# Building a structured matrix by angle addition, and re-timing the loads around it, in a fused S4 + ReGLU training step

## The chip, the cores, the metric

One core of one Trainium2 chip. The metric is the device time of the core in microseconds (us). TensorE is PE in the profile, VectorE DVE, ScalarE ACT, GpSimd POOL, SyncE SP.

## The reference, cut to what matters

`x` is 2048 rows of 576 features. The output is `x` plus two branches of its layernorm, and the kernel returns that output and the gradients of twelve inputs for a given `grad_out`.

```
xn = layernorm(x)
# S4 branch: one long filter per feature, applied by FFT over the rows
dt = exp(log_dt); logdA = dt*(A_re + i A_im); dB = dt*(B_re + i B_im)
K  = Re sum_n C[d,n] * exp(logdA[d,n] * l) * dB[d,n]          # l = 0..2047
y  = irfft(rfft(xn, 4096) * rfft(K, 4096))[:2048] + xn * Dskip
# feed-forward branch, 576 -> 4608 -> 576
h  = relu(xn @ W_gate) * (xn @ W_up);   z = h @ W_down
out = x + y + z
```

## The kernel before: what the change and the argument touch

Two streams of work are written as Python generators and woven into one program. The feed-forward stream runs over 12 chunks of 384 hidden columns and gives PE most of its work. The S4 stream runs beside it: parameters; pass 1 over features 0 to 287 ("half 0"); then making the filter of half 0 beside pass 1 of half 1; making the filter of half 1 beside pass 3 of half 0; pass 3 of half 1. A number that each piece yields, its assumed time, sets the pace at which the two are mixed.

```python
def gen(self):                                   # S4
    yield from self.params()
    self.make_dft16(); yield 1.0
    yield from self.make_dft128()
    with ExitStack() as c:
        pools = self.p2_pools(c)
        yield from self.p1(0)
        yield from self.both(self.p2(0, pools), 0.8 * W2, self.p1(1), W1)
        yield from self.both(self.p2(1, pools), 0.8 * W2, self.p3(0), W3)
    yield from self.p3(1)
    yield from self.grads()                      # parameter gradients, at the end
```

The FFT is split into two steps with a turn through DRAM between them: rows are stored in one order and read in the other. The loads are issued where they are used, with two buffers.

```python
bp = self.pool(c, f"p1_b{hf}", 2)                # pass 1, middle part
for h in range(ST):
    b = bp.tile([P, 2, 2, DH], BF16, name="b_ug")
    nc.sync.dma_start(b[:], self.rows(self.A[2][hf], h))     # the other order
    ...                                          # matmuls (mix)
    Z = self.product(pp, sg[:, 1], sg[:, 0], True)           # DVE
    Ct = bp.tile([P, 1, 2, DH], BF16, name="fC1")
    self.back1(Ct, 0, Z)                                     # matmuls on that product
    nc.sync.dma_start(self.rows(self.C[1][hf], h), Ct[:])
```

The filter needs Y, a complex exponential on a grid of 128 exponents. For four features at a time it is computed directly: angle, range reduction, sine, absolute value, cosine, times the decay.

```python
v.tensor_tensor(E[:], ex[:, es, 16:24]..., ex[:, es, 24:40]..., op=ALU.mult)
v.tensor_tensor(ya[:], par[1]..., qv..., op=ALU.mult)
v.tensor_scalar(yr[:], ya[:], MAGIC, None, op0=ALU.add)
v.scalar_tensor_tensor(yr[:], yr[:], MAGIC, ya[:], op0=ALU.subtract, op1=ALU.subtract)
nc.scalar.activation(sn[:], yr[:], ACT.Sin, scale=-TWO_PI)
nc.scalar.activation(ya[:], yr[:], ACT.Abs)
nc.scalar.activation(cs[:], ya[:], ACT.Sin, scale=-TWO_PI, bias=g.hpcol[:])
v.tensor_tensor(Y[:, 0], Ef, cs[:], op=ALU.mult)
v.tensor_tensor(Y[:, 1], Ef, sn[:], op=ALU.mult)
```

In the feed-forward stream, twelve transposes (three tiles of four) run in a bunch through two PSUM buffers, and the chunk's gate, up and down weights have two copies, loaded half a chunk ahead from ScalarE's queue.

```python
def t_unit(self, c, sg, ft):
    for src, dst in zip(self.T[(c, sg, ft)], (self.hN, self.dgN, self.duN)):
        pt = g.psum_t.tile([P, 8, P], BF16, name="pt")       # pool of 2
        for j in range(JS):
            nc.tensor.transpose(out=pt[:, j, :], in_=src[:, j * P:(j + 1) * P], ...)
        g.bal.copy(dst[...], pt[:, 0:JS, :], 512, fp32=False)    # DVE or ACT

def load_wd(self, c):
    for i in (2, 0, 1):
        self.g.nc.scalar.dma_start(self.wds_[c % 2][:, i], self.Wd_in[c][:, i])
```

## Time and profile before

| | before |
|---|---|
| median, lowest, highest of 4 runs | 1968.49, 1966.09, 1975.11 us |
| span of the profiled run, granted clock | 1971.6 us, 0.978 |
| PE busy, idle | 1799.4, 172.2 us |
| DVE busy, ACT busy | 1412.0, 1355.9 us |

Read the PE row as span minus busy: that idle time is what a change outside PE's own work can reach. The lines themselves, and what is lost inside "busy", are in the prediction below.

### The profile page before, as it was taken

The page shows a single profiled execution, that of the slowest core. Times are in us where ns is not written, and L with a number is a line of the kernel's source. Part 1 is how long each engine was busy: PE and PEld are TensorE (multiplying, and loading weights), DVE is VectorE, ACT ScalarE, POOL GpSimd, SP SyncE. Part 2 cuts the span into 40 slices and gives each one's busy share as a digit, 9 for nine tenths or more (in the row PEclk, how much of TensorE's full clock was granted, in tenths as well). Part 3 has the DMA queues.
Part 4 walks back from the last instruction along what each step waited for, and adds up shares of the span by engine and source line. Part 5 has one row for each costly group of instructions (what it writes and reads, how often), then busy time and mean ns, then how long its engine had stood idle before and what let it go on. Part 6 is the DMA issues. An engine that isn't in the chain of part 4 may idle for free.

```text
span 1971.6 us, 42743 instructions
## 1 busy us (share of the span) xinstructions
PE 1799.4 (91%) x16257; PEld 1225.3 (62%) x16395; DVE 1412.0 (72%) x3521; ACT 1355.9 (69%) x3058; POOL 225.3 (11%) x276
## 2 busy tenths in 40 slices
PE   6879897999999999999899999999999998996999
PEld 3555565556766766766656756766766755564666
DVE  8746772699778688688577887868888833746882
ACT  2775683698779679679668769859868836644342
POOL 2111110012101011011101101101201200100000
PEclk9989998999999999999899999999999999998999
DMA  9688888766756756856856755755755656885874
GB/s 340 204 310 264 238 220 238 230 200 130 222 147 146 229 138 142 240 152 135 227 184 128 196 167 125 181 173 136 181 180 107 158 188 183 204 220 149 276 245 126
DMA packets 205961, 377.62 MB, mean 192 GB/s; under 512 B 34810, under 2 KB 115834, under 8 KB 203706
## 3 DMA queue, kind: packets, MB, share of 16 engines
q1 hardware_dynamic: 172922, 284.35, 44.4%
q0 software_dynamic: 25344, 54.28, 18.5%
q10 hardware_dynamic: 7488, 36.24, 5.2%
q8 instruction: 128, 2.10, 0.4%
q14 instruction: 79, 0.65, 0.1%
HBM read 235.29 MB, written 139.50 MB: 190 GB/s over the span
## 4 chain that ended last, share of the span: by engine, by line
PE 42%; DVE 19%; ACT 19%; DMA 14%; issue 4%; SPq 1%; POOL 0%; ACTq 0%; DVEq 0%; POOLq 0%
PE ps_mm L202 10%; PE ps_mm L250 9%; PE ps_mm L299 9%; PE ps_mm L286 3%; ACT osx L66 3%; DMA rows<-in_gq_dram 2%; PE ps_s L572 2%; PE pt L226 2%; DMA A_k<-fA 2%; ACT YT L66 2%; PE ps_s L806 2%; ACT hN L66 2%; PE ps_s L573 2%; DVE pr L822 1%; DMA bC<-C_dk 1%
## 5 line engine op out<-in xcount | busy, mean ns | idle before, releaser
L202 PE MATMUL ps_mm<-xT,wd 128*128 128x512 bf16 x1308 | 346.9, 384 | 8.0 <-DVE xT L139 1.0
L202 PEld LDWEIGHTS <-wd 128*128 128x128 bf16 x2160 | 204.0, 98 | 200.4 <-issue 14.6
L66 ACT CAST osx<-ps_mm 128x288 bf16<-128x288 f32 x658 | 255.9, 439 | 32.3 <-PE ps_mm L250 31.1
L260 POOL DMA_DIRECT2D acc_dram<-osx x160 | 138.7, 869 | 1156.4 <-ACT osx L66 805.4
L250 PE MATMUL ps_mm<-wf,dgT 128*128 128x288 bf16 x1152 | 215.8, 289 | 12.3 <-ACT osx L66 9.8
L250 PE MATMUL ps_mm<-wf,duT 128*128 128x288 bf16 x1152 | 216.5, 290 | 0.0
L299 PEld LDWEIGHTS <-rows 128*128 128x128 bf16 x1536 | 147.2, 98 | 96.7 <-issue 6.2
L250 PE MATMUL ps_mm<-wf,hT 128*128 128x288 bf16 x1152 | 192.8, 289 | 4.9 <-ACT osx L66 3.6
L202 PE MATMUL ps_mm<-gT,wd 128*128 128x512 bf16 x714 | 183.6, 379 | 0.3
L822 DVE TENSOR_TENSOR pr<-X,ps_s 128x256 f32<-128x256 f32 x288 | 109.1, 415 | 96.2 <-PE ps_s L818 95.0
L286 PE MATMUL ps_mm<-rows,hN 128*128 128x144 bf16 x2304 | 160.9, 231 | 14.2 <-DMA rows<-in_gq_dram 14.0
L286 PEld LDWEIGHTS <-hN 128*128 128x128 bf16 x2304 | 153.4, 100 | 22.7 <-issue 14.4
L209 DVE SCALAR_TENSOR_TENSOR upm<-rg,ps_mm 128x512 bf16<-128x512 bf16 x144 | 98.3, 683 | 92.7 <-PE ps_mm L202 74.0
L66 ACT COPY YT<-ps_s 128x1024 bf16<-128x1024 bf16 x142 | 145.9, 1028 | 26.8 <-PE ps_s L806 24.8
L299 PE MATMUL ps_mm<-dgN,rows 128*128 128x384 bf16 x768 | 144.2, 326 | 0.2 <-ACT rg L207 0.2
L250 PEld LDWEIGHTS <-dgT 128*128 128x128 bf16 x1152 | 112.5, 99 | 44.4 <-issue 14.8
L299 PE MATMUL ps_mm<-duN,rows 128*128 128x384 bf16 x768 | 137.0, 326 | 0.0
L250 PEld LDWEIGHTS <-duT 128*128 128x128 bf16 x1152 | 112.5, 99 | 28.9 <-issue 1.0
L250 PEld LDWEIGHTS <-hT 128*128 128x128 bf16 x1152 | 107.6, 99 | 36.2 <-issue 7.8
L66 ACT CAST dhb<-ps_mm 128x512 bf16<-128x512 f32 x144 | 84.7, 588 | 54.7 <-PE ps_mm L202 54.1
L66 ACT CAST obw<-ps_mm 128x384 bf16<-128x384 f32 x105 | 50.0, 478 | 102.8 <-PE ps_mm L299 83.3
L750 ACT ACTIVATE ycs<-ya,hpcol 128x512 bf16<-128x512 f32 x144 | 107.7, 748 | 2.9 <-DVE Y L753 2.1
(223 smaller groups left out, 3690.3 us busy)
## 6 DMA issues: line engine op xcount, KB each, us to landing
acc_dram<-osx POOLq DMA_DIRECT2D x176, 288.0 KB, 4.7
xT<-xT_dram SPq DMA_DIRECT2D x44, 640.0 KB, 5.4
gT<-in_gT_dram SPq DMA_DIRECT2D x44, 640.0 KB, 6.2
rows<-in_gq_dram SPq DMA_DIRECT2D x48, 576.0 KB, 4.9
rows<-xs_dram SPq DMA_DIRECT2D x48, 512.0 KB, 5.2
wd<-in_Wd_dram ACTq DMA_DIRECT2D x36, 480.0 KB, 6.9
wf<-in_Wf_dram ACTq DMA_DIRECT2D x12, 1296.0 KB, 9.1
ex_dram<-exs SPq DMA_DIRECT2D x18, 640.0 KB, 3.5
```

The costliest lines, as they stand in the source:

```text
L66: self.nc.scalar.copy(out, in_)
L202: nc.tensor.matmul(ps[:], lhsT=w[:, k, fs], rhs=rhs[:, k, :], start=(k == 0), stop=(k == NK - 1))
L209: nc.vector.scalar_tensor_tensor(upm[:], rg[:], 0.0, ps_u[:], op0=ALU.is_gt, op1=ALU.mult)
L226: nc.tensor.transpose(out=pt[:, j, :], in_=src[:, j * P:(j + 1) * P], identity=g.ident_bf[:])
L250: nc.tensor.matmul(ps[:, :DH], lhsT=lt, rhs=rh, start=(i == 0), stop=(i == len(mms) - 1))
L260: nc.gpsimd.dma_start(g.acc_dram[:, t, :, :], o[:], accum_op=ALU.add)
L286: nc.tensor.matmul(ps[:, (ft - f) * 144:(ft - f + 1) * 144], lhsT=self.hN[:, st, ft * P:(ft + 1) * P], rhs=gq[:, st, :], start=(st == 0), ...
L299: nc.tensor.matmul(ps[:, :Fc], lhsT=xs[:, st, 0:P], rhs=src[:, st, :], start=(st == 0), stop=(st == ST - 1))
L572: nc.tensor.matmul(ps[:, :DH], lhsT=CC[:], rhs=src[:, o, :], start=True, stop=False)
L573: nc.tensor.matmul(ps[:, :DH], lhsT=sm[:], rhs=src[:, other, :], start=False, stop=True)
L750: nc.scalar.activation(cs[:], ya[:], ACT.Sin, scale=-TWO_PI, bias=g.hpcol[:])
L822: nc.vector.tensor_tensor(pr[:], X[:, dx:dx + DG, r0:r0 + 2].rearrange("p d r a -> p d (r a)").unsqueeze(2).to_broadcast(sh), psg[:, 0:DG ...
```

## The change

Its intent: cut the work of DVE and ACT in making Y, and take away places where PE stands still for a round trip through DRAM, a PSUM buffer or a queue. Cut to the core (cuts are marked with ...):

```diff
 # making Y: by angle addition, Y = U + V, from small factors A (8 steps) and B (16 steps)
-E, ya, yr, sn, cs, Y as above: 6 DVE and 3 ACT instructions of 512 columns per 4 features
+A = [xop.tile([P, SX, 2, 8, 2], BF16, ...) for i in range(2)]    # once per 16 features
+B = xop.tile([P, SX, 2, 16], BF16, name="B")
+...
+v.tensor_tensor(vw(U), Ap(0), Bp(1), op=ALU.mult)                # per 4 features
+v.tensor_tensor(vw(V), Ap(1), Bp(0), op=ALU.mult)
+v.tensor_tensor(Y[:], U[:], V[:], op=ALU.add)
 # loads run ahead of use; the product of step h and the inverse of step h-1 are interleaved
+class Ahead: ...                       # keeps n loads in flight
-yield from self.p1(0)
+yield from self.both(self.p1(0, 4, 4.0), 68.0, self.params(pw), 45.0)    # depth 4, pause 4.0
-... self.p1(1) ... self.p3(0)
+... self.p1(1, 2, 0.0) ... self.p3(0, 2, 0.0)
-yield from self.p3(1)
-yield from self.grads()
+yield from self.p3(1, 4, 4.0)
 # the second DFT table is turned on PE from the first (32 transposes), not computed
 # the parameters come transposed from the host; gradients follow each filter half
+yield from self.param_grads(hf, Sm, pw, xp, yop)                         # end of p2
 # feed-forward: one bunch of 4 transposes after each group of matmuls
-def t_unit(self, c, sg, ft): ...
+def t_steps(self, units): ... yield
+    for _ in turns: next(src)
 # one copy of the weights, loaded at the chunk's start from SyncE's queue (chunk 0: ScalarE's)
-self.g.nc.scalar.dma_start(self.wds_[c % 2][:, i], self.Wd_in[c][:, i])
+(self.g.nc.scalar if c == 0 else self.g.nc.sync).dma_start(self.wd[i][:], self.Wd_in[c][:, i])
-PACE = 0.9
-W1, W2, W3 = 56.0, 400.0, 62.0
+PACE = 0.86
+W1, W2, W3 = 60.0, 400.0, 58.0
```

The "pause" is a piece of the S4 stream that does nothing: feed-forward work fills it while the store before the turn lands.

## The prediction

Its first rival is that U and V take 1.2 us each, not the 0.69 that it counts on, and load DVE. Its times for DVE's new instructions, and so its 78 us less on DVE, are the author's estimate: no DVE row of the kernel before multiplies or adds 1024 columns. The rows that come nearest allow both figures, again as estimates. In bf16 288 columns take 301 ns (L584) and 576 take 453 (L581), which puts 1024 at some 690 by a straight line; in fp32 512 columns take 684 ns (L743) and 1280 take 1490 (L515), which puts 1024 at some 1220.

Three things that it uses without a row are in the trace of the kernel before. A transpose takes 57 ns and a tiny matmul 24 in a run of eight (it counts 56 and 25):

```profile
1012.52 0.19 PE ps_s L796 x8
1012.71 0.46 PE ps_s L806 x8
```

And one wait cost more than its length: in the 2.7 us after the one of 4.79 us that the prediction shows (124.6 to 127.3 us), the granted clock was 0.50 and three matmuls of 288 columns took 0.88 to 0.92 us; from 128.95 us on three took 0.53 or 0.54. After a wait of 2.04 us at 133.37 us it was 1.00, and they took 0.53.

> **What bounds the kernel now.** I read the page's busy shares first, then the windows view by stage, then TensorE's waits, the chain of waits, the groups by form and one stretch of the timeline.
>
> ```profile
> PE 1799.4 (91%) x16257; PEld 1225.3 (62%) x16395; DVE 1412.0 (72%) x3521; ACT 1355.9 (69%) x3058; POOL 225.3 (11%) x276
> ```
>
> TensorE leads, but a busy PE is not a PE at its peak, so I ask how long its matmuls would take back to back. The chain of waits has dense runs:
>
> ```profile
> 59.38 2.60 PE ps_mm L202 x12
> ...
> 69.81 2.82 PE ps_mm L250 x23
> ...
> 1931.88 12.00 PE ps_mm L286 x192
> 1943.88 20.80 PE ps_mm L299 x128
> ```
>
> That is 216 ns for 512 columns, 123 for 288, 62.5 for 144, 162.5 for 384. Counting from the source: 2160 x 216 = 467 us, 3680 x 123 = 453, 2304 x 62.5 = 144, 1536 x 162.5 = 250, 384 half-width matmuls that run in pairs 31; for the S4 half 1024 x 123 = 126, 2960 transposes x 56 = 166, 2304 tiny ones x 25 = 58. Together 1695 us. The span is 1971.6, so some 277 us are lost: 172 as idle (1971.6 - 1799.4), some 105 inside "busy" (restarts, and a lower granted clock). The windows view says where (columns: stretch, then busy us and count of PE, PEld, DVE, ACT, POOL, then clock, DMA share, GB/s):
>
> ```profile
> 0.00:16.00 16.00, 0.00 (x0) 0.00 (x0) 9.94 (x45) 1.90 (x4) 2.10 (x12) 1.00 0.89 348
> ...
> 100.00:220.00 120.00, 101.72 (x774) 65.20 (x779) 66.58 (x124) 79.42 (x158) 17.25 (x33) 0.96 0.85 286
> 220.00:360.00 140.00, 117.27 (x888) 78.37 (x895) 71.09 (x194) 76.95 (x195) 13.61 (x15) 0.93 0.82 226
> 360.00:940.00 580.00, 551.95 (x5399) 380.79 (x5444) 473.26 (x1112) 470.63 (x1063) 72.11 (x75) 0.99 0.65 173
> ...
> 1000.00:1600.00 600.00, 573.25 (x5643) 399.39 (x5690) 469.88 (x1136) 464.41 (x1043) 76.74 (x80) 1.00 0.63 161
> 1600.00:1760.00 160.00, 147.59 (x1154) 94.62 (x1160) 80.29 (x247) 93.17 (x240) 13.80 (x16) 0.98 0.75 201
> 1760.00:1824.00 64.00, 46.40 (x292) 27.18 (x294) 38.00 (x157) 28.39 (x65) 1.07 (x2) 0.85 0.55 158
> ```
>
> PE idle is 41 us in 100 to 360 (parameters, DFT tables, first S4 pass), 55 in the two long middle stretches, where DVE and ACT are both near 80%, and 30 in 1600 to 1824 (last S4 pass and parameter gradients). What ended PE's idle time:
>
> ```profile
> PE ps_s L602 <- DMA bC<-C_dk: 14.8, 7, 6.9
> PE ps_mm L286 <- DMA rows<-in_gq_dram: 14.0, 8, 3.4
> PE ps_mm L250 <- ACT osx L66: 13.4, 10, 4.8
> PE pt L226 <- ACT hN L66: 13.0, 24, 4.2
> PE ps_s L561 <- ACT fA L66: 12.6, 12, 5.4
> ...
> PE ps_s L98 <- DVE dld L870: 6.3, 1, 6.3
> ```
>
> Latencies, then: a DRAM round trip, a PSUM buffer, an in-order queue behind another's wait. The timeline shows the last kind:
>
> ```profile
> 121.22 3.02 DVE L515 TENSOR_TENSOR exs<-Tt,ev 128x1280 f32<-128x1280 f32 x2 [4.24 <-DMA ex_dram<-exs]
> ...
> 124.68 0.88 PE L250 MATMUL ps_mm<-wf,dgT 128*128 128x288 bf16 x3 [4.79 <-ACT osx L66]
> ```
>
> DVE waits for a store to free exs, ACT's Exp waits for DVE, the PSUM copies of the feed-forward part queue behind that Exp, and PE, which needs their buffers, stands still for 4.79 us.
>
> [...] the gappy stretches have clocks of 0.93 and 0.85, the dense ones 0.99 and 1.00. So a removed gap saves more than its length. [...]
>
> **The change, part by part.** PE's matmuls stay: the instruction streams differ by 32 new transposes of 56 ns and some 40 small ones gone. The 1695 us floor stands, and only the lost 277 can shrink.
>
> *Making Y.* Per four channels the old code spends three ACT and six DVE instructions, among them:
>
> ```profile
> L748 ACT ACTIVATE ysn<-yr 128x512 bf16<-128x512 f32 x144 | 94.7, 658 | 11.7 <-DVE yr L745 10.7 <-DVE Y L754 0.4
> L743 DVE TENSOR_TENSOR ya<-Tt,qv 128x512 f32<-128x512 f32 x144 | 98.3, 684 | 5.8 <-ACT ycs L750 5.4
> ```
>
> All six DVE groups: 98.7 + 98.3 + 61.9 + 98.7 + 66.8 + 60.1 = 484.5 us. ACT's three: 94.7 + 95.1 + 107.7 = 297.5. The new code builds Y by angle addition, Y = U + V, from small factors: 3 x 144 bf16 instructions of 1024 columns[...]. The per-16-channel block grows: angles for 40 exponents instead of 16[...]. Its three ACT instructions grow from 1.43 to 2.39 us by the row slope (256 to 512 columns costs 216 ns): +35. Net: DVE -78, ACT -262.
>
> *Parameters and gradients.* With the host's transposed layout no PE transposes, no R and T round trips, half the trigonometry of the DFT tables: about DVE -30, ACT -20. So DVE ends near 1300, ACT near 1080. This is off PE's path; it shortens the answers to PE.
>
> *Waits.* Idle saved, stage by stage:
> - 60 to 360 (46 us idle): exs gets three buffers and is spread over the first S4 pass; the pass prefetches four deep, pipelines product and inverse by one step, and puts a pause of feed-forward work before each DRAM turn-around. I give 28 of the 46: the store-to-load turn itself remains.
> - Middle (360 to 1600, 65 us with the entry of the second pass at 940 to 1000): feed-forward transposes no longer come three in a row on two PSUM buffers, but one after each matmul group (13.6 us of hN and duN waits); a lighter ACT answers sooner. Against it the gate, up and down weights lose their second copy and load at the chunk's start on SyncE's queue, ahead of the rows that already cost 14.0. I give 20 - 5 = 15.
> - 1600 to 1824 (30 us): the gradients leave the end (6.3 for dld, the R loads, stores at L473 and L849), the last pass prefetches four deep: 18.
> - Final stage (8 us): 2.
>
> Sum 63. Each idle us came with 105/172 = 0.6 us of hidden loss; since part of that is fixed, I take 0.55: 63 x 1.55 = 98. From 1968.5 that gives 1870; with 2 us for the new transposes, **1872 us**, 4.9% less.
>
> **Rivals.**
> [...] Sums and feed-forward products answer later and the middle gains nothing or loses: about 1915. For it: four-dimensional operands with repeats, seen in no row. Against: yE already repeats a word sixteen times at 687 ns, no slower than plain rows[...].
> *Single weights turn into the wait.* 1.44 MB more at each of 11 chunk starts is some 4 us at the 340 GB/s that the page's fullest slices reach. About 20 us of final products and down-gradients lie ahead of first use, so gate and up are hidden, but rows queue behind them. If 2 to 3 us show at each start: +25, about 1895.
> *The middle does not care.* Its idle is 4.5%, in hundreds of short waits, and PE, DVE and ACT share out latency. If only start and end gain, (28 + 18 + 2) x 1.55 = 74: about 1895.
> *More than I think.* If nearly all hidden loss goes and the middle's idle halves: about 1840.
>
> **Range and chances.** The first and last stages alone carry it past the 2% line (1929), whatever the middle does, unless U and V are slow and the weights stall too. 8 in 10: 1838 to 1915. Faster by over 2%: 0.91; within 2%: 0.08; slower: 0.01.
>
> **What would show it.** U, V and Y near 690 ns each (1.2 us refutes it); ACT busy near 1080, DVE near 1300; PE idle near 110 us; the 100 to 360 stretch without a 4 us wait on osx; waits of pt on hN under 4 us; no R or dld row, and final products starting some 90 us earlier. New waits of L200 on wd, or rows waits well above 14 us, would speak for the second rival. If PE idle fell and time did not, the hidden part would be wrong.

## The result, and the profile after

The changed kernel takes **1884.01 us** (median of 10 runs, 1880.80 to 1889.69) against 1968.51 (15 runs, 1966.09 to 1976.94). The ratio is 0.9565, with a 95% interval of 0.9549 to 0.9581: 4.35% less. Ratios here are the mean time of one kernel's fast runs over that of the other's of the same rounds, so not quite the ratio of the medians. All outputs are right.

The profiled run spans 1886.4 us at a clock of 0.988. The page's first part, to be read against the line of before at the head of the prediction:

```profile
PE 1764.8 (94%) x16248; PEld 1218.4 (65%) x16389; DVE 1335.8 (71%) x3059; ACT 1162.0 (62%) x2599; POOL 217.3 (12%) x264
```

PE idle is 1886.4 - 1764.8 = 121.6 us, 50.6 less than before. The span fell by 85.2, so each idle microsecond brought 1.68. ACT is far lighter, DVE a little.

The windows view of the changed kernel (stretch, then busy time and count of PE, PEld, DVE, ACT, POOL, then clock, DMA share, GB/s). The stretches are cut where the S4 stream changes stage in that trace: the first pass writes out its result (dk) at 346 us in the kernel before and at 279 us now.

```profile
0.00:285.00 285.00, 243.92 (x1823) 159.22 (x1845) 199.74 (x505) 176.92 (x385) 41.41 (x78) 0.98 0.85 285
285.00:1510.00 1225.00, 1168.65 (x11460) 815.61 (x11554) 912.79 (x1999) 808.49 (x1814) 159.13 (x167) 0.99 0.66 173
1510.00:1740.00 230.00, 220.74 (x1904) 151.08 (x1919) 130.96 (x353) 121.56 (x295) 16.74 (x20) 0.99 0.76 224
1740.00:1846.00 106.00, 95.01 (x709) 65.71 (x714) 86.87 (x188) 46.21 (x90) 0.00 (x0) 0.97 0.71 221
1846.00:1887.00 41.00, 36.42 (x360) 26.74 (x357) 5.47 (x15) 8.86 (x19) 0.00 (x0) 1.00 0.41 119
```

The same stages of before, as far as the prediction did not show them or cut them elsewhere, in the same columns:

```profile
0.00:350.00 350.00, 286.29 (x2146) 185.98 (x2168) 215.65 (x571) 205.47 (x450) 52.26 (x94) 0.96 0.82 261
350.00:1600.00 1250.00, 1184.01 (x11607) 822.80 (x11702) 981.35 (x2338) 976.46 (x2203) 158.20 (x164) 0.99 0.65 170
1824.00:1932.00 108.00, 99.72 (x725) 68.89 (x731) 91.99 (x198) 43.78 (x84) 0.00 (x0) 0.96 0.80 250
1932.00:1972.00 40.00, 35.40 (x350) 25.86 (x347) 4.72 (x11) 8.69 (x17) 0.00 (x0) 1.00 0.42 119
```

From such lines, length minus PE busy for each stage, the account of the idle time follows (rows are rounded; the sums are those of the two pages):

| stage (before / after, us) | idle before | idle after | saved | predicted |
|---|---|---|---|---|
| start, 0–350 / 0–285 | 63.7 | 41.1 | 22.6 | 28 |
| middle, 350–1600 / 285–1510 | 66.0 | 56.4 | 9.6 | 15 |
| last pass and gradients, 1600–1824 / 1510–1740 | 30.0 | 9.3 | 20.7 | 18 |
| final stage, 1824–end / 1740–end | 12.5 | 15.0 | -2.5 | 2 |
| sum | 172.2 | 121.6 | 50.6 | 63 |

The stretches hold different amounts of feed-forward work, so their idle time compares, but not their length. A cut at 360 us in both traces, where the prediction drew its line, would count some 7 us of waits at the entry of the changed kernel's second pass (290 to 302 us) to the start.

What PE waited for in the changed kernel (us in total, times, longest):

```profile
PE ps_s L585 <- DMA bC<-C_dk: 10.0, 6, 6.9
PE ps_s L544 <- ACT fA L66: 9.0, 8, 5.2
PE pt L227 <- DVE dgT L216: 7.8, 5, 3.6
PE ps_s L555 <- DMA b_ug<-A_ug: 7.7, 2, 6.9
...
PE ps_mm L290 <- DMA rows<-in_gq_dram: 2.1, 4, 0.8
...
PE pt L227 <- ACT hN L66: 1.6, 2, 0.9
...
PE ps_mm L253 <- ACT osx L66: 0.2, 1, 0.2
```

The waits for rows (14.0 before) and for osx (13.4) are down to 2.1 and 0.2. The copies of hN have nearly vanished as a releaser, but dgT has come up, and 6.9 of its 7.8 us lie between 1740 and 1846: the final stage. The turns through DRAM are shorter in sum, not gone. One long wait for C_dk is new. It lies in the second pass, where the kernel before lost only 1.1 us to C_dk; most of the 14.8 us of before was in the first pass (13.6). In the timeline's columns (start and length in us, engine, line, instruction, in brackets the idle time before it):

```profile
782.43 0.64 PE L585 MATMUL ps_s<-bC,Sx 128*128 128x288 bf16 x2 [6.87 <-DMA bC<-C_dk]
```

Summed over all rows of this view, ACT released 60.3 us before and 22.0 now, DMA 51.0 and 28.4, DVE 41.2 and 52.7.

The groups by form for the new operations (busy us, mean ns of one, then idle time before them):

```profile
L766 DVE TENSOR_TENSOR Y<-U,V 128x1024 bf16<-128x1024 bf16 x144 | 110.3, 766 | 13.2 <-PE ps_s L801 12.6
L764 DVE TENSOR_TENSOR V<-A,B 128x1024 bf16<-128x1024 bf16 x144 | 101.2, 703 | 0.0
L763 DVE TENSOR_TENSOR U<-A,B 128x1024 bf16<-128x1024 bf16 x144 | 98.5, 684 | 1.0
```

U and V are within 2% of the 690 ns that the prediction named, repeats and all. So is Y in the median, as its tile's view shows (count, then min/median/max ns, first and last start in us):

```profile
L766 DVE TENSOR_TENSOR Y<-U,V x144: 671/684/2777, 251.5 to 1550.0; 128x1024 bf16<-128x1024 bf16 x144
```

Nine of the 144 took 1.2 to 2.8 us, each while a GpSimd instruction ran; they lift the mean to 766.

Where the lead was won can be read from the end of each chunk's last weight-gradient matmul, the one of half width, in both traces. "Lead" is the time of before minus that of the run, in us, at the end of chunks 1, 3, 4, 5, 9, 10 and 11 (counted from 0; e1 to e10 are explained below). Each row is one profiled run, and runs of one kernel differ by several us (1880.80 to 1889.69 for the changed kernel). A lead counts feed-forward work alone: a run that has done less S4 work by then leads only until that work comes.

| run | c1 | c3 | c4 | c5 | c9 | c10 | c11 |
|---|---|---|---|---|---|---|---|
| changed kernel | 28.7 | 35.3 | 30.4 | 47.0 | 58.0 | 67.3 | 85.0 |
| e1 ACT load | 25.1 | 22.6 | 11.6 | 25.0 | 35.6 | 47.0 | 64.3 |
| e2 bunched | 34.9 | 43.4 | 35.8 | 50.8 | 57.4 | 67.7 | 90.2 |
| e3 shallow | 22.1 | 30.5 | 31.9 | 42.1 | 49.1 | 42.9 | 58.4 |
| e5 parameters first | 17.2 | 23.6 | 19.3 | 36.1 | 46.0 | 58.6 | 76.1 |
| e6 depth 2, pauses kept | 22.4 | 32.2 | 26.9 | 43.7 | 54.2 | 53.2 | 67.2 |
| e8 GpSimd in the final stage | 27.3 | 34.7 | 31.4 | 48.3 | 58.1 | 67.1 | 93.2 |
| e10 before, single weights | 6.7 | 6.2 | 6.8 | 7.8 | 14.4 | 12.1 | 15.5 |

For the changed kernel: some 35 us by the end of chunk 3, 23 from there to chunk 9, and 27 in the last two chunks. Of the middle's 23, 16.6 come in chunk 5 alone, which in the kernel before holds the entry into pass 3 (its gappy stretch 940 to 1000); chunk 4, which holds the new wait for C_dk, lost 4.9, and chunks 6 to 9 brought 11.

### The profile page after: what moved, and what is told of

Its sections match the earlier page's. It is cut to its first block, busy times and chain, and to the rows that moved or that the text cites. A ratio compares the mean times of both kernels' runs of the same rounds, so it can differ in the third digit from the quotient of the medians.

```text
span 1886.4 us, 41680 instructions
## 1 busy us (share of the span) xinstructions
PE 1764.8 (94%) x16248; PEld 1218.4 (65%) x16389; DVE 1335.8 (71%) x3059; ACT 1162.0 (62%) x2599; POOL 217.3 (12%) x264
## 5 line engine op out<-in xcount | busy, mean ns | idle before, releaser
L200 PE MATMUL ps_mm<-xT,wd 128*128 128x512 bf16 x1304 | 351.2, 382 | 7.1 <-DVE osx L60 0.9
L200 PEld LDWEIGHTS <-wd 128*128 128x128 bf16 x2160 | 197.9, 98 | 167.4 <-issue 11.7
L66 ACT CAST osx<-ps_mm 128x288 bf16<-128x288 f32 x677 | 259.2, 418 | 61.1 <-PE ps_mm L253 58.4
L253 PE MATMUL ps_mm<-wf,duT 128*128 128x288 bf16 x1152 | 210.2, 288 | 0.0
L817 DVE TENSOR_TENSOR pr<-X,ps_s 128x256 f32<-128x256 f32 x288 | 119.9, 416 | 105.6 <-PE ps_s L813 102.7
L303 PE MATMUL ps_mm<-duN,rows 128*128 128x384 bf16 x768 | 132.7, 326 | 0.0
L818 DVE TENSOR_REDUCE Sm<-pr 128x8 f32<-128x256 f32 x288 | 119.1, 414 | 3.6
```

What stands on the lines that cost most here:

```text
L66: self.nc.scalar.copy(out, in_)
L200: nc.tensor.matmul(ps[:], lhsT=w[:, k, fs], rhs=rhs[:, k, :], start=(k == 0), stop=(k == NK - 1))
L253: nc.tensor.matmul(ps[:, :DH], lhsT=lt, rhs=rh, start=(i == 0), stop=(i == len(mms) - 1))
L303: nc.tensor.matmul(ps[:, :Fc], lhsT=xs[:, st, 0:P], rhs=src[:, st, :], start=(st == 0), stop=(st == ST - 1))
L817: nc.vector.tensor_tensor(pr[:], X[:, dx:dx + DG, r0:r0 + 2].rearrange("p d r a -> p d (r a)").unsqueeze(2).to_broadcast(sh), psg[:, 0:DG ...
L818: nc.vector.tensor_reduce(out=Sm[:, vi, s0 + dd:s0 + dd + DG, :], in_=pr[:], op=ALU.add, axis=AX.X)
```

## The experiments

All twelve are edits of the changed kernel, except e10, and all were timed in rounds against the kernel before on the same chip. e1 to e4 shared one chip and its runs of before, e5 to e8 a second, e9 to e12 a third; on which chip the changed kernel's own ten runs were is not on record. So differences to it are differences of ratios: (ratio - 0.9565) x 1968.5.

| run | median us | ratio to before (95%) | against the changed kernel |
|---|---|---|---|
| e1_act_back | 1904.77 | 0.9667 (0.9645–0.9689) | +20 us |
| e2_bunched | 1888.05 | 0.9578 (0.9552–0.9604) | +3, not told apart |
| e3_shallow | 1915.81 | 0.9719 (0.9692–0.9746) | +30 |
| e4_uv_slow | 1894.62 | 0.9614 (0.9591–0.9637) | +10 |
| e5_params_first | 1895.91 | 0.9623 (0.9586–0.9660) | +11 |
| e6_depth2_pause | 1904.91 | 0.9663 (0.9617–0.9709) | +19 |
| e7_grads_end | 1898.42 | 0.9636 (0.9598–0.9674) | +14 |
| e8_final_g | 1877.33 | 0.9528 (0.9490–0.9566) | -7 |
| e9_all_back | 1956.23 | 0.9941 (0.9906–0.9976) | +74 |
| e10_before_wd1 | 1956.38 | 0.9934 (0.9907–0.9960) | before -0.66% |
| e11_best | 1878.72 | 0.9536 (0.9511–0.9562) | -6 |
| e12_best_gap | 1886.89 | 0.9580 (0.9556–0.9605) | +3 |

My theory was that the gain is a sum of removed waits of different kinds: the start's spread and prefetch, ACT's relief, the order of the transposes, the last pass. The rivals: DVE's speed is what matters; or the weights cost what the rest gains; or the middle does not care.

### e1: give ACT its work back

```diff
+for fn, kw in ((ACT.Sin, {}), (ACT.Abs, {}), (ACT.Sin, dict(bias=g.hpcol[:])), (ACT.Abs, {})):
+    jb = jp.tile([P, 384], BF16, name="jb")
+    nc.scalar.activation(jb[:], pw[:, 1, 0:384], fn, scale=-TWO_PI, **kw)    # per 4 features, unread
```

(The fp32 identity matrix, used only at the start, moved to another pool to make room.)

> The changed kernel with ScalarE's old load put back: four activations of 384 columns per four channels, written to a tile that nobody reads (some 144 x 4 x 0.55 = 317 us of instructions). Theory A (a freed ScalarE answers TensorE's PSUM waits sooner, and this pays for the middle): 20 to 35 us slower than the changed kernel, that is 1904 to 1919 us, with TensorE's waits for ScalarE back from 22 to some 45 us or more. Theory B (the order of the transposes and the prefetches pay, ScalarE was never in the way): under 8 us slower, 1892 us at most, waits for ScalarE under 30 us. Either way ScalarE busy near 1400 us.

It cost 20 us. The page of e1:

```profile
PE 1765.6 (93%) x16248; PEld 1216.1 (64%) x16389; DVE 1336.6 (70%) x3059; ACT 1398.7 (73%) x3175; POOL 217.1 (11%) x264
```

PE and DVE are as in the changed kernel, ACT is near the level of before (1355.9), so the total is about right. PE's waits for ACT rise from 22.0 to 46.7 us, as theory A said. But the place of the load is not that of before. The view of the added tile (count, then min/median/max ns, first and last start in us) shows it:

```profile
L768 ACT ACTIVATE jb<-pw x432: 505/527/807, 288.3 to 1052.6; 128x384 bf16<-128x384 f32 x144
```

The activations depend on nothing but the parameters, and they were drawn forward: all had started by 1052.6 us, while the products for Y (U) go on until 1568.9. One stretch of the windows view, first of the kernel before, then of the changed kernel, then of e1 (ACT's busy time is the fourth pair):

```profile
360.00:650.00 290.00, 275.04 (x2670) 187.24 (x2693) 246.05 (x584) 243.08 (x560) 35.14 (x36) 0.99 0.67 179
```

```profile
360.00:650.00 290.00, 279.16 (x2754) 195.10 (x2774) 213.65 (x466) 198.34 (x453) 38.20 (x40) 0.99 0.69 180
```

```profile
360.00:650.00 290.00, 271.48 (x2673) 189.19 (x2694) 206.25 (x449) 278.26 (x653) 38.07 (x40) 1.00 0.67 179
```

ACT is at 96% there, against 84% before. The table of leads agrees: e1 loses 19 us against the changed kernel by the end of chunk 4, 22 by chunk 5, and nothing more once the load has stopped. So e1 shows that ACT's load in the middle costs PE time when ACT is nearly full; that taking the old load away was worth the same 20 us at its old density of 84% is not shown, and 20 may be too much.

### e2: transposes in bunches again

```diff
-            for _ in turns:
-                next(src)
+        for _ in src: pass          # all three groups of four after the unit's matmuls
```

> The changed kernel with the feed-forward transposes in bunches again, behind a unit's matmuls and ahead of a dx unit. Theory B: 12 to 20 us slower (1896 to 1904), with waits of the transposes on ScalarE's copies back near 13 us. Theory A: with a lighter ScalarE the bunches are drained in time anyway; under 6 us slower (1890 at most).

The intervals overlap, and +3 is what theory A allowed (under 6). By the leads the profiled run, the fastest of its four, was even ahead of the changed kernel's for most of the way. Yet the waits view shows the removed wait returned, as theory B had said:

```profile
PE pt L227 <- ACT hN L66: 12.6, 27, 1.5
```

In exchange the 11 us for dgT and hT before transposes are gone (DVE's releases fall from 52.7 to 37.1 us). The spread order takes one wait and brings another of the same size. A reason would be that each group of transposes now comes sooner after the product that it turns; that was not tested.

### e3 and e6: shallow loads, with and without the pauses

```diff
-p1(0, 4, 4.0) ... p3(1, 4, 4.0)
+p1(0, 2, 0.0) ... p3(1, 2, 0.0)     # e3
+p1(0, 2, 4.0) ... p3(1, 2, 4.0)     # e6
```

> The changed kernel with two instead of four buffers in the first and last S4 passes and without their pauses of 4 us. Theory C (prefetch and pauses pay at the start and the end): 15 to 30 us slower (1899 to 1914), with TensorE's waits for DMA up from 28 us by 10 or more. Rival (the software pipelining of product and inverse and the spread of the parameters do it): under 6 us slower.

> The changed kernel with two buffers in the first and last pass but the pauses of 4 us kept; the shallow run had neither and took 1916. If the depth pays, this stays near 1916 (1908 or more). If the pauses pay, it comes back to 1884 to 1893.

e3 costs 30 us, the upper end of what theory C said, and DMA's releases rise from 28.4 to 40.5 us. e6 costs 19 and falls between its two outcomes, so both parts pay: the depth of four about 19, the pauses some 10 more. The second figure is the weaker one, since the intervals of e3 and e6 overlap (0.9692 to 0.9709). In e3 a wait of the feed-forward part comes back from 2.1 us, though its code is untouched:

```profile
PE ps_mm L290 <- DMA rows<-in_gq_dram: 13.1, 9, 4.3
```

The leads place e6's loss against the changed kernel: 6 us at chunk 1, of which half comes back by chunk 3, then 14 of the final 18 in the last two chunks (10 in chunk 10). So the deep prefetch pays most in the last pass.

### e4: U and V made slow

```diff
-B = xop.tile([P, SX, 2, 16], BF16, name="B")
+B = jp.tile([P, SX, 2, 16], F32, name="B")
```

> The changed kernel with factor B held in fp32, [...] both should go from 0.69 to about 1.22 us, VectorE's busy time from 1336 to about 1460 us. If VectorE is the next bound after TensorE (TensorE's waits for it are now the largest, 53 us): 25 to 45 us slower (1909 to 1929). If the middle does not care about VectorE: under 8 us slower.

The groups of e4:

```profile
L764 DVE TENSOR_TENSOR V<-A,B 128x1024 bf16<-128x1024 bf16 x144 | 178.9, 1242 | 0.0
L763 DVE TENSOR_TENSOR U<-A,B 128x1024 bf16<-128x1024 bf16 x144 | 175.7, 1220 | 0.7
```

This is what the first rival of the prediction described, to within 2% of the 1.22 us written down for it, and DVE's busy time rises from 1335.8 to 1484.6. The cost is 10 us, between the two outcomes written down (under 8, 25 to 45), and not the 43 that the rival put on it. DVE has room here (busy 71% of the span in the changed kernel); that U and V take 684 and 703 ns, not 1220 and 1242, is worth 10 us, and not what the gain hangs on.

### e5 and e7: where the parameters and their gradients are done

```diff
-yield from self.both(self.p1(0, 4, 4.0), 68.0, self.params(pw), 45.0)    # e5
+yield from self.params(pw)
+yield from self.p1(0, 4, 4.0)
```

> The changed kernel with the parameters made ahead of the first S4 pass, as in the kernel before, not woven into it. Theory (the weaving hides the exs stores and the pass's DRAM turns): 8 to 20 us slower, 1892 to 1904. Rival (three exs buffers were enough): within 5 us of 1884.

```diff
 # e7: e6, and the gradients of half 1 behind the last pass
+                yield from self.p3(1, 2, 4.0)
+                yield from self.param_grads(*self.last)
```

> As the run with two buffers and pauses, with the gradients of the second half of the channels moved behind the last pass. Theory (the gradients' place at the end cost the kernel before some 10 to 20 us): 4 to 12 us slower than the run with two buffers and pauses, since the new form has no DRAM round trip of R and half of it stays early. Rival: within 3 us.

Spreading the parameters over the first pass is worth 11 us, all of it by the end of chunk 1 (lead 17.2 against 28.7). Putting the gradients back to the end costs nothing: e7 is 6 us faster than e6, of the same job (1894.98–1901.38 against 1900.50–1906.92), which neither statement for e7 had said. The prediction had booked the gradients' removal from the end as one of three things that its 18 us there come from. What is shown to pay there is the prefetch of the last pass. e7 moved one half of the gradients in their new form; that form itself, without the trip through DRAM and the 6.3 us wait for dld, was not undone, so what it brings is not shown.

### e8: the final stage

The account above shows the final stage as the only one that got worse, with DVE busy 82% of it (85% before). The base product was moved to GpSimd, idle there:

```diff
-            self.pool = pool("fin3", 3)
+            self.pool = pool("fin3", 4)
-        nc.vector.tensor_tensor(base[:], xg[:], self.dsk..., op=ALU.mult)
-        g.bal.add(d=1.2)
+        nc.gpsimd.tensor_tensor(base[:], xg[:], self.dsk..., op=ALU.mult)
```

The 6 us a piece in what was expected is an estimate: 16 products in the 106 us of the stage leave 6.6 us each. The queue on SyncE is in the changed kernel's trace: from 1700 to 1846 us it stood 19.0 us, in six waits, before the load of xt (L934) until a matmul was done.

> A trial to beat the changed kernel: in the final stage four buffers instead of three with the same look-ahead, so that the loads do not queue on SyncE behind the last tile's use, and the base product (1.36 us x 16 on VectorE) on idle GpSimd. TensorE lost about 11 us there, 7 of it on dgT behind VectorE. Expected 4 to 12 us faster, 1872 to 1880; if GpSimd is slower than some 6 us a piece it turns into the wait and the time stays at 1884 or rises.

The tile's own row, then the same 106 us of the final stage in the windows view, of e8:

```profile
L941 POOL TENSOR_TENSOR f_base<-f_xg,dsk x16: 2358/2366/2653, 1709.0 to 1826.6; 128x1152 f32<-128x1152 bf16 x16
```

```profile
1732.00:1838.00 106.00, 100.23 (x779) 70.75 (x786) 86.81 (x187) 49.22 (x95) 28.69 (x12) 1.00 0.73 227
```

PE idle there is 5.8 us in place of 11.0, the wait for dgT in the whole run falls from 7.8 to 0.9, and the lead grows from 67.1 to 93.2 in the last two columns of the table, against 67.3 to 85.0. e8 is 7 us faster than the changed kernel by the ratios. The two ratios' intervals overlap (0.9549 to 0.9566) and they ran in different jobs, so the size is uncertain; e11 below, with the same edit in a third job, gives 6. The fourth buffer came with it and is not told apart from the move. Nor is it shown that a lighter DVE is the reason: its busy time in these 106 us did not fall (86.87 and 86.81). Single DVE instructions on this tile took up to 2.79 us (L971) and 2.81 us (L974) in e8, with medians of 0.76 and 0.82; in the changed kernel, where GpSimd is idle in this stage, the longest of the same two operations (L972, L975) took 0.76 and 0.82.

### e9 and e10: is it all there, and what do the weights do alone

e9 undoes e1, e2, e3 and e5 together. e10 is the kernel before with the weights' part of the change alone:

```diff
-        self.wds_ = [wp.tile([P, 3, NK, Fc], BF16, ...) for i in range(2)]
+        self.wd = [wp.tile([P, NK, Fc], BF16, ...) for i in range(3)]
-            self.g.nc.scalar.dma_start(self.wds_[c % 2][:, i], ...)      # half a chunk ahead
+            (... scalar if c == 0 else ... sync).dma_start(self.wd[i][:], ...)   # chunk start
```

> The changed kernel with four parts undone at once: ScalarE's load put back (+21 alone), two buffers and no pauses (+32), parameters ahead of the first pass (+12), bunched transposes (+4). If they add up they give +69: 1953 us. If they share waits (a wait removed by one is hidden by another), it comes out below: 1930 to 1945. If they feed each other (bunches hurt only a loaded ScalarE), above 1960. What is left to the 1969 of the kernel before is the rest of the change (lighter VectorE, pipelined passes, weights, gradients).

> The kernel before with only the weights' change: gate, up and down weights in one copy, loaded at the chunk's start on SyncE's queue. The rival of the prediction (rows and first matmuls queue behind the loads): 15 to 30 us slower than the kernel before, 1984 to 1998, with rows waits above 20 us. Theory from the trace after the change (no matmul waited for wd, rows waited 2 us): within 8 us of 1969, either way.

e9 is 74 us slower than the changed kernel; the four parts one by one make 20 + 3 + 30 + 11 = 64. So they add up roughly, with no large sum hidden in their interplay. What stays of the gain in e9, 0.59%, is as large as what the weights alone bring to the kernel before, 0.66%. Read with care: e9 carries e1's load, which ran from 120 to 942 us, so it too has ACT fuller than the kernel before ever had it. The near equality therefore does not prove that the lighter DVE, the interleaved product and the transposed parameters bring nothing.

e10 was the surprise: single weights, loaded when they are nearly due, make the kernel faster. Its waits, against 14.0 and 13.4 before:

```profile
PE ps_mm L286 <- DMA rows<-in_gq_dram: 9.2, 6, 2.5
PE ps_mm L250 <- ACT osx L66: 8.8, 6, 2.9
```

And the issues of those loads in the kernel before, on ScalarE's queue (count, then min/median/max ns):

```profile
L180 ACTq DMA_DIRECT2D wd<-in_Wd_dram x36: 334/335/719, 0.8 to 1579.5; - x36
```

All but chunk 0's three, that is 33 issues of 335 ns or 11 us, have left the queue that also makes the PSUM copies. The 13 us gained are of that size, and the wait for osx fell. But the transfers moved in time as well, and the two were not separated: why it gains stays open.

### e11 and e12: looking for more

e11 is e8 with the gradients of half 1 behind the last pass (depth four kept). e12 adds longer pauses:

```diff
-p1(0, 4, 4.0) ... p1(1, 2, 0.0) ... p3(1, 4, 4.0)
+p1(0, 4, 8.0) ... p1(1, 2, 5.0) ... p3(1, 4, 6.0)      # e12
```

> The changed kernel with the final stage's trial (1877 us alone) and the second half's gradients behind the last pass, which stays four deep. The run with the gradients at the end gained 6 us over its neighbour. If both gains add: 1869 to 1874. If the gradients' place does not matter once the pass is four deep: 1875 to 1880.

> As the run before, with longer pauses of feed-forward work ahead of the DRAM turns: 8 for 4 in the first pass, 5 for none in the second, 6 for 4 in the last. TensorE still lost 7 us at each of two turns (b_ug of the first, C_dk of the second pass). If pauses cover them: 6 to 12 us faster than the run before, 1860 to 1868. If the turns are bound by the stores' own queue: within 3 us.

e11 is no better than e8 (1878.72 against 1877.33). e12 is 8 us worse than e11, of the same job, which neither of its outcomes had allowed. The pauses did cover the turns: PE's waits for C_dk fall from 10.0 us in the changed kernel to 2.4, for b_ug from 7.7 to 3.0. In its trace the lead is 71.0 at the end of chunk 5, 24 more than the changed kernel's, but 69.3 after chunk 10: longer pauses stretch the S4 stream, and what they gain early is paid back where it ends later. The best versions found are e8, 1877.33 us, 0.9528 of the kernel before, and e11, not told apart from it.

## Why the prediction was right, and where its steps were off

Predicted 1872 us (1838 to 1915), faster at 0.91; measured 1884.01, faster. The time lies in the range, 12 us above the predicted value.

- **What bounds the kernel.** Right. PE's work did not change and no other engine became the bound; the gain is PE's lost time alone.
- **Idle and the factor.** 63 us of idle were to go, 50.6 went; the time that idle brings beside itself was put at 0.55 x 63 = 35, and came to 85.2 - 50.6 = 34.6. That this part fits is luck: the factor was 34.6 / 50.6 = 0.68 and made up for the idle that stayed. With 0.55 the 50.6 would have brought 78 us, not 85. The terms of the 63: the start was over-sized ("28 of the 46": 22.6, counted from 0), so was the middle ("20 - 5 = 15": 9.6), the final stage had the wrong sign ("2": -2.5), and the end ("18": 20.7) was slightly low. At the start the turn through DRAM remains (6.9 us for b_ug in one wait), as the prediction itself said. In the middle the second pass has a wait of the same length for C_dk, which no term of the prediction allowed for.
- **The middle was made of other things than were booked.** 13.6 us of transposes' waits were to go: the waits went, but others of the same size came, and e2 finds nothing to tell. The weights were charged 5 us and bring 13 by themselves to the kernel before (e10). And most of the middle's gain in time lies in one place, the entry into pass 3 in chunk 5. The rival "the middle does not care" was thus about as close as the prediction: its 1895 is 11 us above the measured time, 1872 is 12 below it.
- **The end.** The size held; of its named causes the prefetch is borne out (e6: 14 us in the last two chunks), the gradients' place is not (e7, e11), and their new form was not tried alone.
- **Making Y.** U and V were predicted near 690 ns and ran at 684 and 703; Y took 684 in the median, 766 in the mean. With B in fp32 U and V took 1220 and 1242 (e4). The rival of slow operands was excluded by the trace, and its price was four times too high.
- **DVE and ACT busy.** Predicted near 1300 and 1080, measured 1335.8 and 1162.0. The work itself was well counted: the durations of all instructions sum to 115 us less on DVE and 314 less on ACT, against 108 and 282. But neighbouring instructions of an engine overlap in the records, and the page's busy time counts an overlap once: on ACT before, 1661 us of durations make 1355.9 busy. Subtracting groups' sums from that figure overstates its fall. Nothing in the time hung on it.
- **The weights as a new wait.** Refuted: rows waits fell to 2.1 us, and alone the edit gains.
- **The signs named in advance.** The 4 us wait for osx is gone, hN is under 4 us, no dld or R row is left, and the final products start 90 us earlier (1737.3 against 1827.2); PE idle is 121.6, not near 110.

Open: the value of ACT's relief at its old density; whether the weights gain by the issue queue or by the place of the transfers; what the lighter DVE, the interleaved product and the gradients' new form bring; whether e8 gains by GpSimd or by its fourth buffer.

## What to carry to other kernels

Account for a change by stage: idle time of the bounding engine, before and after, in stretches that mean the same, cut at each trace's own stages; it shows in one table which term of a sum was wrong and which stage got worse, and that stage (here the final one) is a place to look next. A wait that vanishes from the list has not saved anything until an undo shows it in the time: the transposes' wait went and others of its size took its place, and e12 shortened two long waits and lost 8 us. And when an experiment adds load, look in its trace for where the load ran: in e1 the load depended on nothing but the parameters, all of it had started by 1052.6 us while U went on to 1568.9, and so it tested another thing than was meant.

## Times of single instructions in these runs

- In both kernels' streams 512 columns took 216 ns on PE (12 in 2.60 us, in the chain shown in the prediction; five in 1.08 us in that of the changed kernel), each with its own weight load. In the changed kernel one transpose lasts 219 ns in the median, and since they overlap, the chain has eight in 0.45 us, 56 ns each:

```profile
1734.29 0.45 PE pt L227 x8
```

- One issue of a weight load held ScalarE's queue for 335 ns in the kernel before, 33 of them 11 us, on an engine whose copies of osx PE waited 13.4 us for; the edit that moved them (with the loads' place) gained 13 us.
- Sums of groups' times must not be subtracted from an engine's busy time: 1661 us of ACT durations are 1355.9 us of busy time in the kernel before.
- e8's GpSimd product (1152 columns, bf16 to fp32) took 2366 ns, against 1358 on VectorE in the changed kernel. (Spans on GpSimd are rough in this profile.)
